# Constant operand for idle products, V0 and V1 in two units each, tile 0 transposed on TensorE, in a scheduled transformer block

## Chip, core and metric

One core of one Trainium2 chip runs the whole program. The metric is the device time in microseconds (us) of an execution, the median of several. Most executions agree within 0.3%, so differences of 0.1 or 0.2 us out of 274 are read from the trace, where single instructions are placed to a few nanoseconds, and only larger ones from the times. PE is TensorE, PEld its weight loads, DVE VectorE, ACT ScalarE, POOL GpSimd, SP the engine that issues most DMAs. PSUM is the memory, in eight banks, that TensorE writes its products to. A "look" is one profiled execution.

## The reference

x is 2048 tokens by 640, taken as 16 tiles of 128 tokens. Cut to what matters:

```python
xn  = layernorm(x)                       # per token, no weights
qkv = xn @ wqkv                          # 640 x 1920; 32 heads of 20
phi = softmax of +-(q @ w_phi), +-(k @ w_phi)   # per head
kv, z = phi_k.T @ v, sum(phi_k)
att = (phi_q @ kv) / (phi_q @ z + 1e-6) @ wo
mlp = (silu(xn @ w1) * (xn @ w3)) @ w2   # 640 -> 1536 -> 640
out = x + att + mlp
```

## The kernel before

The kernel is a program that writes a program. Every instruction is entered with a model duration and its inputs, a list scheduler fixes each engine's order (with random tie-breaking from a seed up to 175 us of model time), and the order is then emitted with semaphore waits. So one edit can move much else.

TensorE is the engine that sets the time. It can't start on real work until x has landed and a tile has been centred, and it starts at half clock; therefore the scheduler fills its first gaps with idle products ("filler"), which nobody reads:

```python
TURNED = (0,)                 # tiles whose normalised rows are transposed by DMA
SEED = 385
...
zero = new("zero", [128, 512], bf, RH + 12288)
...
def consts():
    memset("DVE", warm[:], 0.0, 19)
    memset("DVE", zero[:], 0.0, 9)
    zeroed.append(P.all[-1])
...
def filler(t, until):
    ...
    while t < until:
        cold = t < 5.2
        n = 512 if until - t > 0.5 else 128
        c = n / (1200 if cold else 2400)
        def emit(n=n):
            return nc.tensor.matmul(bank(u.k, n), zero[:, 0:128], zero[:, 0:n], start=True, stop=True)
        P.mm(emit, [], 0, c, n)
        P.all.pop().raw = set(zeroed)      # waits for the memset
        t += c
```

The first four tiles take a short path to V. A tile is centred (`xc`: its mean from an ACT sum, or from DVE's statistics for tile 3), transposed on TensorE (`cT0` to `cT3`), copied from PSUM to `xcT` by ACT or DVE, and multiplied by wv (`V0` to `V3`, ten products of 320 columns each); the copy out of PSUM multiplies by the inverse deviation. Besides, the normalised tiles are transposed into `xnT` (`xT1` to `xT3` on TensorE, tile 0 by DMA). V0 and V1 stand in one piece:

```python
def v_pair(t, level):
    both = P.begin(4, level, stream="V")
    for a, b, u in ((0, 3, 0), (0, 3, 1), (3, DC, 0), (3, DC, 1)):   # chunks a..b of tile t+u
        ...
        for i in range(a, b):
            for q in range(2):
                mm(2 * u + q, ..., xcT[:, t + u, i, :], wv[:, i, 320 * q:320 * q + 320], i == 0, i == DC - 1)
...
P.schedule({"PE": 1.25, "ACT": 1.12, "DVE": 0.93, "POOL": 0.8, "SP": 0.81}, filler, 12.0, SEED, 175.0)
```

The softmax here doesn't subtract the row's maximum and nothing guards it: scores larger than these inputs give would overflow.

## Time and profile before

| | before |
|---|---|
| median time | 274.41 us (3 runs, 274.11 to 274.45) |
| span of the profiled execution | 272.6 us |
| first idle product | 1.29 us |
| clock released (record, and product spacing) | 7.14 us |
| cT0, V0, cT2, V2 start | 4.68, 6.49, 8.98, 10.31 us |
| first MLP product to last product | 14.14 to 269.82 us |

The prediction below shows the shares, the chain and the tile views. One more view: the timeline of the stretch ahead of V2 (columns: start us, length us, engine, line, operation, output<-input, shapes, count, and in brackets the idle time before it and what ended it). These are chosen lines of the kernel before:

```profile
7.33 0.73 ACT L628 ACTIVATE junk<-x_tok 128x640 bf16<-128x640 bf16 x1
...
8.19 0.39 DVE L628 TENSOR_SCALAR xc<-x_tok,mv 128x640 bf16<-128x640 bf16 x1 [0.83 <-ACT junk L628]
...
8.98 0.44 PE L811 MATMUL PS<-ident,xc 128*128 128x128 bf16 x5
...
9.46 0.49 DVE L628 COPY xcT<-PS 128x640 bf16<-128x640 bf16 x1
...
9.80 0.67 PE L1094 MATMUL PS<-zero 128*128 128x128 bf16 x9
...
10.31 1.52 PE L620 MATMUL PS<-wv,xcT 128*128 128x320 bf16 x10
```

Tile 2's sum on ACT, its centring on DVE, its transposes cT2, its copy and V2 form a chain, and TensorE spends the end of it in nine idle products. And V2's operand is copied by 9.95 (9.46 + 0.49) while V2 starts at 10.31: more than half of the idle block comes after the data is there.

### The profile page before, as it was taken

What the parts mean: (1) busy time and instruction counts of PE and PEld (TensorE: products, weight loads), DVE (VectorE), ACT (ScalarE), POOL (GpSimd) and SP (SyncE); (2) the same over time, 40 slices, a digit from 0 to 9 for tenths busy, and PEclk for the clock granted to TensorE, in tenths of its full rate; (3) what the DMA queues carried; (4) which work ended last, traced back from release to release, by engine and by line L of the source; (5) the groups of instructions that cost most, each with busy time, mean ns of one, the idle gap of its engine ahead of it and who ended that gap; (6) DMA issues with size and microseconds to landing.
All of it is one profiled execution on the core that took longest, in us unless ns stands there. A gap on an engine that the chain in (4) does not pass through costs nothing.

```text
span 272.6 us, 5091 instructions
## 1 busy us (share of the span) xinstructions
PE 268.8 (99%) x2099; PEld 159.9 (59%) x2099; DVE 183.8 (67%) x326; ACT 104.2 (38%) x193; POOL 60.5 (22%) x101
## 2 busy tenths in 40 slices
PE   8999999999999999999999999999999999999996
PEld 4747446777754448444444446677677774444774
DVE  5748998999999443588969795677673215666112
ACT  5637754776754540356663354100110002222000
POOL 3320552689999900000000000000000000000000
PEclk9999999999999999999999999999999999999999
DMA  7968996763000000803111111433353222000001
GB/s 233 183 95 258 345 216 129 118 175 114 2 0 2 0 0 10 284 1 46 29 26 24 24 26 25 98 100 96 90 107 83 64 75 72 0 0 0 26 24 48
DMA packets 41959, 22.14 MB, mean 81 GB/s; under 512 B 27728, under 2 KB 41936, under 8 KB 41936
## 3 DMA queue, kind: packets, MB, share of 16 engines
q1 hardware_dynamic: 41360, 21.17, 32.6%
q10 hardware_dynamic: 576, 0.66, 0.7%
q8 instruction: 16, 0.26, 0.4%
q14 instruction: 7, 0.06, 0.1%
HBM read 12.81 MB, written 2.62 MB: 57 GB/s over the span
## 4 chain that ended last, share of the span: by engine, by line
PE 99%; DVE 0%; issue 0%
PE PS L620 96%; PE PS L1094 2%; PE PS L811 1%; PE PS L865 0%; DVE xres L628 0%; DVE zero L628 0%; DVE warm L628 0%
## 5 line engine op out<-in xcount | busy, mean ns | idle before, releaser
L620 PE MATMUL PS<-xnT,w_s 128*128 128x512 bf16 x480 | 106.7, 379 | 0.0
L620 PEld LDWEIGHTS PS<-xnT,w_s 128*128 128x128 bf16 x480 | 46.6, 98 | 55.2
L620 PE MATMUL PS<-w_s,hT 128*128 128x320 bf16 (+2 forms) x384 | 55.0, 300 | 0.0
L628 ACT ACTIVATE th<-PS 128x512 f32<-128x512 f32 x48 | 28.7, 597 | 68.8 <-PE PS L620 68.8
L628 DVE SCALAR_TENSOR_TENSOR t<-th,PS 128x512 bf16<-128x512 f32 x48 | 32.7, 684 | 29.8 <-ACT th L628 29.8
L620 PEld LDWEIGHTS PS<-w_s,hT 128*128 128x128 bf16 x384 | 36.9, 98 | 14.8
L628 POOL TENSOR_TENSOR ekt<-ekt,rS 128x640 bf16<-128x640 bf16 x32 | 39.4, 1268 | 0.7 <-DVE rS L628 0.7
L628 DVE TENSOR_TENSOR xres<-PS,xres 128x640 bf16<-128x640 f32 (+2 forms) x17 | 13.4, 786 | 36.9 <-PE PS L620 36.9
L628 DVE SCALAR_TENSOR_TENSOR hT<-t,PS 128x512 bf16<-128x512 bf16 x48 | 32.7, 683 | 1.3
L628 ACT ACTIVATE EqT<-PS 128x512 bf16<-128x512 f32 x40 | 21.8, 594 | 11.3 <-PE PS L620 11.3
L628 ACT ACTIVATE e_s<-PS 128x64 f32<-128x64 f32 x32 | 9.1, 283 | 40.6 <-PE PS L620 40.1
L620 PE MATMUL PS<-wo_s,oT 128*128 128x320 bf16 (+2 forms) x160 | 24.5, 299 | 0.0
L628 DVE TENSOR_TENSOR prod<-PS,g_s 128x1280 bf16<-128x1280 f32 x16 | 23.9, 1492 | 0.6
L620 PE MATMUL PS<-Wkp,xnT 128*128 128x320 bf16 x160 | 23.9, 299 | 0.0
L628 ACT ACTIVATE ekt<-PS 128x640 bf16<-128x640 f32 x32 | 20.7, 698 | 7.5 <-PE PS L620 7.3
L620 PE MATMUL PS<-xnT,Wqp 128*128 128x512 bf16 x100 | 23.4, 380 | 0.0
L628 DVE TENSOR_REDUCE S<-ekt 128x64 f32<-128x1280 bf16 x16 | 22.9, 1449 | 0.0
L620 PEld LDWEIGHTS PS<-wo_s,oT 128*128 128x128 bf16 x160 | 15.7, 98 | 6.1
L620 PEld LDWEIGHTS PS<-Wkp,xnT 128*128 128x128 bf16 x160 | 15.5, 98 | 5.9
L620 PE MATMUL PS<-wv,xnT 128*128 128x320 bf16 x120 | 18.3, 299 | 0.0
L628 DVE BATCH_NORM_STATS2 bst<-x_tok 128x6 f32<-128x320 bf16 x32 | 13.9, 464 | 2.9 <-DMA x_tok<-in_A_x_dram 2.9
L620 PEld LDWEIGHTS PS<-xnT,Wqp 128*128 128x128 bf16 x100 | 9.3, 98 | 10.8
(68 smaller groups left out, 171.0 us busy)
## 6 DMA issues: line engine op xcount, KB each, us to landing
w_s<-in_B_w_dram SPq DMA_DIRECT2D x8, 480.0 KB, 7.7
xres<-in_A_x_dram SPq DMA_DIRECT2D x16, 160.0 KB, 2.2
out_dram<-xres SPq DMA_DIRECT2D x15, 160.0 KB, 1.8
x_tok<-in_A_x_dram SPq DMA_DIRECT2D x3, 640.0 KB, 7.5
w_s<-in_B_w_dram SPq DMA_DIRECT2D x1, 1920.0 KB, 9.1
wo_s<-in_A_wo_dram SPq DMA_DIRECT2D x1, 800.0 KB, 4.7
x_tok<-in_A_x_dram SPq DMA_DIRECT2D x2, 160.0 KB, 3.4
x_tok<-in_A_x_dram ACTq DMA_DIRECT2D x2, 160.0 KB, 3.8
```

Source lines behind the costliest of these rows:

```text
L620: return nc.tensor.matmul(o(u.k), l, r, start=start, stop=stop, skip_group_check=shared)
L628: return getattr(e, name)(*[at(a, u) for a in args], **{k: at(v, u) for k, v in kw.items()})
L811: return nc.tensor.transpose(PSb[:, a:a + 128], l, ident[:])
L1094: return nc.tensor.matmul(bank(u.k, n), zero[:, 0:128], zero[:, 0:n], start=True, stop=True)
```

## The change

The intent is to get TensorE through its preparation sooner. Idle products read a constant that the preamble sets anyway (1.0, one column per partition, read with step zero), so they wait for nothing and start earlier; V0 and V1 are cut into chunks 0 to 2 and 3 to 4, so that V0 can begin before tile 1 is there; tile 0 goes through TensorE like its neighbours. The core of the diff (a centring mode that is not used, and small changes of model durations, are cut):

```diff
-TURNED = (0,)
-SEED = 385
+TURNED = ()
+SEED = 1023
...
-        memset("DVE", zero[:], 0.0, 9)
-        zeroed.append(P.all[-1])
...
+    ones = nc.const_aps.tensor(1.0, [128, 512], bf)
     def filler(t, until):
-            cold = t < 5.2
-            n = 512 if until - t > 0.5 else 128
-            c = n / (1200 if cold else 2400)
+            n = 512 if until - t > 0.9 else 128
+            c = n / (1200 if t < 6.5 else 2400)
-                return nc.tensor.matmul(bank(u.k, n), zero[:, 0:128], zero[:, 0:n], start=True, stop=True)
+                return nc.tensor.matmul(bank(u.k, n), ones[:, 0:128], ones[:, 0:n], start=True, stop=True)
-            P.all.pop().raw = set(zeroed)
+            P.all.pop()
...
-    v_pair(0, 6e4)
+    v_split(0, 6e4 + 20, 6e4 - 8, 3)      # V0a at this level, V0b at the second
+    v_split(1, 6e4 - 5, 6e4 - 9, 3)
...
-    P.schedule({"PE": 1.25, ...
+    P.schedule({"PE": 0.8, ...
```

The second arguments of `v_split` are levels: a higher level goes first when several units could start.

## The prediction

> **What bounds the kernel now.** I read the page first (shares, then the chain of work that ended last), then that chain in order of time, then the timeline of the first 15 us, then the tile views of that stretch.
>
> ```profile
> PE 268.8 (99%) x2099; PEld 159.9 (59%) x2099; DVE 183.8 (67%) x326; ACT 104.2 (38%) x193; POOL 60.5 (22%) x101
> PE 99%; DVE 0%; issue 0%
> ```
>
> The first line is the page's busy time by engine, the second its chain of work by engine: TensorE sets the end from start to finish. Busy time of pipelined matmuls can hide gaps, so I also added up the start-to-start spacing of the single matmul records. From 14.14 us, where the gated MLP begins, to the last matmul at 269.82 us, spacing beyond columns over 2.4 GHz plus 2.5 ns comes to about 2.2 us; some 1.9 us of it are about twenty steps of 95 ns or so each at the change from whole-array to half-array products, which the change leaves alone. So after 14 us there is nothing to win. Before it, the chain in order of time reads:
>
> ```profile
> 0.96 0.28 DVE zero L628
> 1.29 3.60 PE PS L1094 x11
> 4.88 0.54 PE PS L811 x5
> 5.42 0.74 PE PS L1094 x4
> 6.16 0.53 PE PS L811 x5
> 6.70 2.45 PE PS L620 x16
> 9.15 0.28 PE PS L811 x5
> 9.43 0.54 PE PS L620 x4
> 9.97 0.50 PE PS L1094 x9
> 10.47 1.36 PE PS L620 x10
> 11.83 0.28 PE PS L811 x5
> 12.11 0.84 PE PS L865 x15
> 12.95 119.14 PE PS L620 x945
> ```
>
> Columns: start, length, what. L1094 is the idle products on the zero tile, L811 the transposes of a centred tile (cT0 to cT3), L865 the transposes of normalised tiles 1 to 3, L620 real products (V first). The chain counts by ends, about 0.2 us later than the matmul starts. The reader is to see that TensorE is never empty after 1.29 us, but that two blocks of idle products sit between real work: 0.74 us after cT0 and 0.50 us before V2. Those two blocks, and half speed, are all that can be recovered. Half speed is in the tile views of xc and wv (min/median/max ns):
>
> ```profile
> L811 PE MATMUL PS<-ident,xc x20: 219/267/315, 4.7 to 11.9; 128*128 128x128 bf16 x20
> L620 PE MATMUL PS<-wv,xcT x40: 298/299/475, 6.5 to 14.0; 128*128 128x320 bf16 x40
> ```
>
> A cold 128-column product lasts 315 ns, a warm one 219; the single records are spaced 107 and 56 ns (320 columns: 267 and 136 ns). The clock record and the spacing both change at 7.14 us.
>
> **What the Trainium skill says.** "TensorE: Matmul & The Clock Gate", Part 1, says that the array starts at half clock, that a full busy window of about 3.4 us releases it, and that the window is free-running, so the moment varies from run to run. The trace agrees in size: idle products start at 1.29 us, full speed comes at 7.14 us, 5.85 us later; windows of 3.41 us that end at 7.14 would also end at 3.73, and the one ending there would have been busy only from 1.29. No run yet shows the variation. The same page, "Back-to-back issue gap", gives N/1.2 cold and N/2.4 + 2.5 ns warm: 107 and 56 ns for 128 columns, as measured here. "DMA: Bandwidth & Descriptors", section "DMA Transpose (X-bar)", says that TensorE is the alternative way to transpose, into PSUM, with an identity at hand; this trace shows the price of both: the DMA transpose of tile 0 was issued at 6.52 and landed 6.4 us later, one tile on TensorE takes five products of 56 ns and one copy out of 0.49 us (VectorE) or 0.70 us (ScalarE).
>
> **The change part by part.** As nothing after 14.14 us moves in sum, what counts is the start of the MLP. From the first product of cT0 (4.68) to 14.14 are 9.46 us, and the parts account for them: real work at full speed 35 transposes x 0.056 + 40 V products x 0.136 = 1.96 + 5.43 = 7.39; idle products 0.747 + 0.503 = 1.25; extra for half speed 10 transposes x 0.051 + about 0.32 in the first three V products = 0.83. Sum 9.47.
>
> (a) Idle products without a memset. The zero tile is written by VectorE from 0.96 to 1.24 us (the chain above), and TensorE waits for it until 1.29. A preset constant needs no wait; ScalarE starts at 0.80 and VectorE at 0.88, so I expect TensorE at about 0.85 to 0.9, 0.4 us sooner. This moves no real work: cT0 waits for x (landed 3.15), ScalarE's sum (0.74 + 0.19), and the centring of 0.39, over at 4.42. It brings the release of the clock forward by 0.4 us on average, in steps of 3.4 us depending on the phase. Half of real work's cold time is lost, so about -0.2 us on average, 0 if the phase is as in this trace and the earlier window still is not full. The operand's value and its zero step I count as free.
>
> (b) Finer idle products. cT0's operand is ready at 4.42, cT0 starts at 4.68 behind idle products: about -0.15 with small last ones. cT1's operand is ready at 5.28, and cT1 starts at 5.96: one 427 ns product and three of 107 are too many, because the schedule counted them at full speed from 5.2 us while the chip was at half until 7.14. The new boundary, 6.5 us, and the new size limit, 0.9, should let cT1 start near 5.5. About -0.35; but V0 then waits for the copy of xcT0 (5.45 + 0.49 = 5.94), and its first product will come at 6.1 to 6.2 in place of 6.49, so of the two I keep -0.3 in all.
>
> (c) V0 and V1 in two units each. The old pair had to run as one piece of 20 products after both tiles. Now chunks 0 to 2 of V0 need only xcT0 and wv chunks landed at 4.67 and 5.05; chunks 3 and 4 (landed 6.76 and 7.03) come later. So V0 starts before xcT1 is there, the transposes of tile 2 can go between, and the copies of xcT1 and ScalarE's sum for tile 2 (7.33 to 8.15 before) move up some 0.5 us. That sum ends the wait of VectorE for xc2 (0.83 us idle before 8.19), which fed cT2 at 8.98, whose copy ended at 9.95, which is what V2 waited for behind the 0.50 us of idle products. With cT2 half a microsecond earlier that block should go: -0.5.
>
> (d) Work that moves up lands in the cold time: about 0.35 us of it at half speed, +0.17.
>
> (e) Tile 0 on TensorE: five products, +0.28, and one copy of 0.5 to 0.7 us that stands beside work. The removed DMA transpose landed at 12.88, before the MLP's start, and hid fully; removing it saves TensorE nothing.
>
> Sum: -0.2 - 0.3 - 0.5 + 0.17 + 0.28 = -0.55 us. 274.41 - 0.55 = 273.86; I say 273.9, with the MLP starting near 13.6.
>
> **The rivals.** First, the freed engine work does not reach V2: x tile 2 landed only at 6.14 and tile 3 at 7.27, and VectorE is busy almost without a break from 3.17 us to 13.5. If the copies and statistics come in another order, the 0.5 us block comes back elsewhere, and (e) eats the rest: 274.3 to 274.5. For it speaks that VectorE did 2.46 us of work in the 3.31 us from 6.49 to 9.80; against it, that 0.83 of the rest was one wait for ScalarE. Second, the phase of the clock window decides: with the window just filled by the earlier start, the clock would be free at about 4.3 us, no real product is cold, (d) vanishes and 1 us is won: 273.1 to 273.4. For it, PE starts early enough to fill 0.4 us more of the window; against it, phase is chance, and the three times before lie within 0.34 us of each other, less than a random phase would let me expect. Third, the new seed and the earlier model start reshuffle the order up to 175 us; a list that is off by some hundred nanoseconds against the chip stalls TensorE. Now there is only some 0.15 us of such stalls around 21 to 23 us; if a new list has a bad place, +0.3 to +1 us: 274.5 to 275. Against it, the DMA and the other engines have slack (VectorE 67%, ScalarE 38%).
>
> **Range and chances.** The middle is the sum; the low end is the sum with a favourable window (another 0.7 off), the high end the first rival with a little of the third: 273.1 to 274.6. For 2% the time would have to move 5.5 us, while everything before the MLP that is not real work is 4.9 us of starting time (data not there) and 2.1 us of idle and cold: faster by 2% cannot come from this, slower only from a broken schedule. Faster 0.01, same 0.98, slower 0.01.
>
> **What would show it.** Right: the first idle product near 0.9 us with no VectorE memset before it; V's first product near 6.1; no block of idle products between V1 and V2; five more L865-type transposes, no DMA transpose of tile 0 near 6.5; MLP's first product at 13.4 to 13.8; unchanged length from there to the end, 258.5 us. Wrong: an idle block of half a microsecond at 8 to 12 us, a first MLP product after 14, cold spacing (267 ns) past 7.5 us, or single stalls over 0.2 us inside the MLP stretch.

## The result, and the profile after

The changed kernel took 273.99 us (273.73 to 274.42, 6 runs) against 274.32 us (273.46 to 274.52, 6 runs) for the kernel before. Ratios here divide the mean time of one kernel's fast runs by that of the other's fast runs of the same rounds, so they are not quite the ratio of the medians. This one is 0.9994 with a 95% interval of 0.9979 to 1.001: the same, and no gain resolved. Two controls of the unaltered changed kernel, run later beside experiments, gave 1.0004 (0.9976 to 1.0032) and 0.9991 (0.9973 to 1.001).

In the page of the changed kernel the shares look different, but most of that is missing records:

```profile
PE 267.7 (98%) x2082; PEld 159.9 (59%) x2101; DVE 181.2 (66%) x325; ACT 104.4 (38%) x194; POOL 60.8 (22%) x101
...
PE 94%; ACT 2%; DVE 2%; issue 1%
...
L619 PE MATMUL PS<-xnT,w_s 128*128 128x512 bf16 x465 | 105.1, 379 | 1.1 <-issue 0.3
```

The program has 480 of these MLP products, as before, and the trace has 465 records. Where one is missing, the spacing shows a hole of exactly one product (216 ns), and the chain of work wanders off to ACT or DVE in its place. Allowing for that, the first MLP product, whose own record is missing, starts one V spacing after the last V product: 13.925 + 0.136 = 14.06 us. The last product starts at 269.74. So the stretch from MLP to end is 255.68 us, to 5 ns the same as before, and the whole gain of this execution is 14.14 - 14.06 = 0.08 us. The chain in order of time (start, length, what; L1098 idle products, L814 cT, L867 xT, L619 real products):

```profile
0.84 4.00 PE PS L1098 x15
4.84 0.53 PE PS L814 x5
5.37 0.64 PE PS L1098 x6
6.01 1.27 PE PS L619 x6
7.29 0.28 PE PS L814 x5
7.57 0.54 PE PS L619 x4
8.11 0.04 issue
8.15 0.99 PE PS L619 x6
9.14 0.28 PE PS L814 x5
9.42 0.54 PE PS L619 x4
9.96 0.28 PE PS L867 x5
10.24 1.51 PE PS L619 x10
...
14.28 13.59 PE PS L619 x99
```

Three things are as intended: idle products begin at 0.84, V0's first part (6.01) stands before tile 1's transposes (7.29), and the idle block before V2 is gone. And yet V2 starts at 10.22, 0.09 us earlier than before. The timeline says why:

```profile
4.90 0.39 DVE L627 TENSOR_SCALAR xc<-x_tok,mv 128x640 bf16<-128x640 bf16 x1
...
5.95 1.00 PEld L619 LDWEIGHTS PS<-wv,xcT 128*128 128x128 bf16 x6 [0.20 <-ACT xcT L627]
...
7.12 0.44 PE L814 MATMUL PS<-ident,xc 128*128 128x128 bf16 x5
...
7.60 0.49 DVE L627 COPY xcT<-PS 128x640 bf16<-128x640 bf16 x1 [0.67 <-PE PS L814]
...
8.01 0.38 DVE L627 TENSOR_SCALAR xc<-x_tok,mv 128x640 bf16<-128x640 bf16 x1
...
8.15 0.66 PEld L619 LDWEIGHTS PS<-wv,xcT 128*128 128x128 bf16 x6 [0.37 <-DVE xcT L627]
...
8.98 0.44 PE L814 MATMUL PS<-ident,xc 128*128 128x128 bf16 x5
...
9.46 0.70 ACT L627 ACTIVATE xcT<-PS 128x640 bf16<-128x640 bf16 x1 [0.51 <-PE PS L814]
...
10.22 1.53 PE L619 MATMUL PS<-wv,xcT 128*128 128x320 bf16 x10
```

cT1, whose operand was ready at about 5.3, ran at 7.12, behind V0a. So xcT1 was copied at 8.09, V1a waited for it (0.37 us of idle weight loads), cT2 came at 8.98 as in the kernel before, although its operand was ready at 8.4, and V2 waited for its copy. That copy had also changed its engine: ACT took 0.70 us, to 10.16, where DVE had taken 0.49, to 9.95. So the idle block went, but 0.21 us of what that freed went to the slower copy. With a copy as short as before, V2 could have followed the five transposes of tile 0, at 10.08 (an estimate from the product spacing; no run moved this copy back). From V2's start to MLP's start TensorE then has the same 3.84 us of work in both kernels.

The working of the prediction from cT0 to MLP, redone on the changed kernel (single records): real work 40 transposes x 0.056 + 40 V products x 0.136 = 7.67; six idle products 0.64; three holes without any product, before V0a, V1a and V2, 0.15 + 0.21 + 0.14 = 0.50; cold extra 0.26 for five transposes and 0.35 for three V products = 0.61. The sum is 9.42 against 9.43 measured (4.633 to 14.061); the kernel before had 7.39 + 1.25 + 0.83. Idle products became holes, and the five new transposes took the rest.

### The profile page after: what moved, and what is told of

It reads as the page before. It is cut to its first block, busy times and chain, and to the rows that moved or that the text cites. A ratio compares the mean times of both kernels' runs of the same rounds, so it can differ in the third digit from the quotient of the medians.

```text
span 272.5 us, 5069 instructions
## 1 busy us (share of the span) xinstructions
PE 267.7 (98%) x2082; PEld 159.9 (59%) x2101; DVE 181.2 (66%) x325; ACT 104.4 (38%) x194; POOL 60.8 (22%) x101
## 4 chain that ended last, share of the span: by engine, by line
PE 94%; ACT 2%; DVE 2%; issue 1%
PE PS L619 92%; ACT EqT L627 2%; PE PS L1098 2%; DVE S L627 1%; DVE rS L627 1%; PE PS L814 1%; PE PS L867 0%; DVE Wqp L627 0%; DVE xres L627 0%
## 5 line engine op out<-in xcount | busy, mean ns | idle before, releaser
L619 PE MATMUL PS<-xnT,w_s 128*128 128x512 bf16 x465 | 105.1, 379 | 1.1 <-issue 0.3
L619 PEld LDWEIGHTS PS<-xnT,w_s 128*128 128x128 bf16 x480 | 46.4, 98 | 54.6
L619 PE MATMUL PS<-w_s,hT 128*128 128x320 bf16 (+2 forms) x384 | 55.0, 299 | 0.0
L619 PEld LDWEIGHTS PS<-w_s,hT 128*128 128x128 bf16 x384 | 37.1, 98 | 14.9
L627 DVE TENSOR_TENSOR xres<-PS,xres 128x640 bf16<-128x640 f32 (+2 forms) x17 | 13.4, 786 | 40.8 <-PE PS L619 40.8
L619 PE MATMUL PS<-wo_s,oT 128*128 128x320 bf16 (+2 forms) x160 | 24.5, 299 | 0.0
L619 PE MATMUL PS<-Wkp,xnT 128*128 128x320 bf16 x160 | 23.9, 299 | 0.0
L619 PE MATMUL PS<-xnT,Wqp 128*128 128x512 bf16 x96 | 22.9, 380 | 0.3 <-issue 0.2
L619 PEld LDWEIGHTS PS<-wo_s,oT 128*128 128x128 bf16 x160 | 15.7, 98 | 6.1
L619 PEld LDWEIGHTS PS<-Wkp,xnT 128*128 128x128 bf16 x160 | 15.5, 98 | 5.9
L619 PE MATMUL PS<-wv,xnT 128*128 128x320 bf16 x120 | 18.3, 299 | 0.0
L619 PEld LDWEIGHTS PS<-xnT,Wqp 128*128 128x128 bf16 x100 | 9.3, 98 | 10.8
```

Of the source, the lines that this page charges most:

```text
L619: return nc.tensor.matmul(o(u.k), l, r, start=start, stop=stop, skip_group_check=shared)
L627: return getattr(e, name)(*[at(a, u) for a in args], **{k: at(v, u) for k, v in kw.items()})
```

## The experiments

My theory after the result: (1) the gain at V2 was lost because cT1 was put behind V0a; (2) tile 0's five transposes cost nothing, as they stand in V2's wait; (3) the clock is released a fixed 5.85 us after the first product, since both profiles show exactly that (1.29 to 7.14 and 0.84 to 6.69). Rivals: the split itself, or the seed, or weights that land late, or DVE's chain is what holds V2; and for (3), a window that runs free of the kernel's start.

Rescheduling after every edit would move everything else too. So most experiments keep the scheduler's result: the order of each engine is frozen, single instructions are taken out, put in or moved, and the waits are derived anew from the data and PSUM dependences. A build of the frozen kernel without edits gave the same order on every engine. All variants gave correct results.

### Idle products on the zero tile again

```diff
+    ones = zero tile, memset by DVE after warm
+    every idle product waits for that memset
-    the first idle product of 512 columns
```

> The changed kernel with its instruction order frozen, but the idle products read the zero tile again, wait for its memset, and the first long one is dropped so that cT0 stays near 4.65 us. Theory (the clock is released a fixed 5.85 us after the first product, as in both profiles: 1.29 to 7.14 and 0.84 to 6.69): release at 7.14, about 0.45 us more of V0 at half speed, MLP's first product at 14.28 in place of 14.06, time +0.2 us on the changed kernel. Rival (the window runs free of the kernel's start, the two equal distances are chance): release anywhere between 4.7 and 8.1 us, MLP's start not tied to it by 0.2 us.

Measured: 274.08 us, ratio to before 0.9999 (0.9956 to 1.0042). First product at 1.29, but the clock released at 4.02 us, 2.73 us after it. The theory of a fixed distance fell with the first look. The rival's idea stood, but not its range: 4.02 lies before the 4.7 that I had set as the earliest, because I had taken a full window as needed. And there was a second lesson: here no real product ran cold, x landed 0.28 us later than in the changed kernel's profile (DVE's first statistics at 3.46 in place of 3.18), and MLP started at 13.99 in place of 14.06. A clock released 2.7 us sooner (4.02 against 6.69) came with a V2 only 0.08 us sooner. Late data had a part in that: besides x, the last weights of V landed at 7.76 only, and V0b's last two products waited for them until 7.80.

### The idle products alone, in the kernel before

```diff
 kernel before, order frozen
-    memset of the zero tile and the waits for it
+    idle products on the constant 1.0, one more of 512 columns in front
```

> The kernel before with its order frozen and only one part of the change: idle products on the preset constant, no memset, one long idle product more so that cT0 stays near 4.64 us. Theory: first product at 0.84, release at 6.69, V's first products cold for 0.45 us less, MLP at 13.92 in place of 14.14: this part alone wins all that the whole change won (0.08 us in the profile) and more, so the other parts together cost 0.1 us. Rival (the idle products' part is worth nothing, the split did it): release and MLP's start as before, 7.14 and 14.14.

Measured: 273.90 us, ratio 0.9992 (0.9955 to 1.0028). First product at 0.84, release at 6.34, V2 at 10.08, MLP at 13.91 in place of 14.14. The position of MLP came out as expected, partly by luck: the release came 0.80 us sooner than before, 0.35 more than the start did, and one look can't say how much of the 0.80 is due to the start at all and how much to the phase of the window. In its profile this part alone does better than the whole change (13.91 against 14.06). The times don't resolve such a difference.

### No idle products at all

```diff
 changed kernel, order frozen
-    all 21 idle products
```

> The changed kernel, order frozen, with no idle products at all: TensorE first works at cT0, near 4.5 us. Theory (fixed distance): release near 10.3 us, all of V0 and V1 at half speed, MLP at 15.3 to 15.6, time +1.3 to +1.5 us. Rival (free-running window of 3.41 us): release anywhere between 7.9 and 11.3 us. Second rival (idle products are worth nothing because the data waits hide the cold clock): time as the changed kernel.

Measured: 275.17 us, ratio 1.0048 (1.0009 to 1.0088). First product 4.55, release at 9.20, so 4.65 us later: neither fixed nor beyond the rival's range. V0 began at 5.84, and V2 came at 11.16 and MLP at 15.01, 0.95 us later than with idle products. They are worth about 1 us to this kernel by the profiles, less than the 1.3 to 1.5 I had put on them, as the release came 1.1 us sooner than I had set. The times agree: the interval of this ratio excludes 1. The second rival (idle products worth nothing) is out.

### Tile 0 by DMA again

```diff
 changed kernel, order frozen
-    xT0: five transposes on PE, one copy on DVE
+    one DMA transpose on SP behind the first MLP weights
```

> The changed kernel, order frozen, with tile 0 transposed by DMA again (five products and one copy out less, one DMA transpose more). Prediction's step (e): tile 0 on TensorE costs 0.28 us, so MLP at 13.78. Theory now: the five products stand in the wait of V2 for the copy of xcT2 (9.80 to 10.22 us in the changed kernel's profile), so V2 still starts at 10.2 and MLP at 14.06, difference 0 to 0.05 us; VectorE has 0.48 us less to do and gains nothing on the end.

Measured: 274.25 us, ratio 1.0006 (0.9969 to 1.0042); V2 at 10.28, MLP at 14.12. Without the five products nothing came sooner. The chain of this run in order of time shows that V2 waits for the copy on ACT, not for TensorE:

```profile
1.25 4.98 DMA wv<-in_A_wqkv_dram
6.23 0.14 issue
...
9.20 0.29 PE PS L814 x5
9.50 0.02 issue
9.52 0.71 ACT xcT L627
10.23 0.05 issue
10.28 1.53 PE PS L619 x10
```

It also shows a new limit on V0's early start: in this execution the first weights of V landed at 6.23 us only, and V0 started at 6.37 in place of 5.96. The prediction's +0.28 for tile 0 is thus wrong in the changed kernel, because its products stand in a wait.

### cT1 first

```diff
 changed kernel, order frozen
-    PE:  cT0, 6 idle, V0a, cT1, V0b, V1a, cT2, V1b, xT0, V2
+    PE:  cT0, 1 idle, cT1, V0a, V0b, V1a, cT2, V1b, xT0, V2
-    DVE: apply0, aggr1, stats2, copy xcT1
+    DVE: copy xcT1, apply0, aggr1, stats2
```

> The changed kernel, order frozen but for two moves: the transposes of tile 1 (cT1) go before V0's first part (as the prediction had assumed), with one idle product left ahead of them, and VectorE copies xcT1 before it normalises tile 0. Theory: the gain that the prediction put on the block before V2 was lost because cT1 stands behind V0a, so that xcT1 is copied at 8.09 only, V1a and cT2 wait for that (cT2 at 8.98, as before the change), and V2 waits for the copy of xcT2. With cT1 first: cT1 at 5.4, xcT1 copied at 6.6, cT2 near 8.5, V2 at 9.7 in place of 10.2, MLP at 13.5 to 13.8 (14.06), from MLP's start to the last product 255.68 us as in all runs so far, time 0.3 to 0.5 us under the changed kernel. Rival (VectorE's chain for tile 3 or a landing of weights binds anyway): V3 not before 12.6, MLP at 14.0.

Measured: 274.00 us, ratio 0.9976 (0.9951 to 1.0001). V2 at 9.75, MLP at 13.59, 0.47 us ahead of the changed kernel's profile. The edit is one package: cT1's place, five idle products less, and the copy of xcT1 earlier on DVE; the shares of the three were not separated. Run again beside a control of the changed kernel:

> The same kernel as the run with cT1 first, beside the control on one chip: 0.3 to 0.5 us under the control, MLP at 13.5 to 13.7. If the gain in that run was only an early clock release or luck, it lies within 0.15 us of the control.

Measured: 273.72 us, ratio 0.9997 (0.9970 to 1.0024), beside the control

> The changed kernel unaltered, as the control on the same chip. Expected: 0.0 to 0.35 us under the kernel before; MLP's first product 13.9 to 14.2, varying with the moment of the clock's release (so far from 2.7 to 5.9 us after the first product) and with the landing of x and of the V weights; 255.7 us from there to the last product.

with 274.20 us, 1.0004. MLP stood at 13.25 here (record missing, one spacing after the last V product) and at 14.22 in the control. The means of the six runs are 273.87 and 274.11, so 0.24 us, less than the 0.3 to 0.5 expected and not resolved: single runs of the first reach from 273.53 to 274.74. In both looks at this kernel the clock happened to be released early (spacing turns near 4.7 and 4.4 us), so part of the distance to the control is chance. The fair partner is the zero-tile run, with the old order, a release at 4.02 and MLP at 13.99. In it and in the first look V0b waited for its last weights (landed at 7.76 and 7.37), which leaves 0.40 us for the order at an early clock. In the second look these weights had landed by 6.98 and nothing waited for them, so its 0.74 us holds the luck of an early landing too.

The lines of the timeline for the first look, which answer to those of the changed kernel:

```profile
5.75 0.45 PE L814 MATMUL PS<-ident,xc 128*128 128x128 bf16 x5 [0.53 <-ACT xcT L627]
...
6.24 0.49 DVE L627 COPY xcT<-PS 128x640 bf16<-128x640 bf16 x1 [0.15 <-PE PS L814]
...
8.51 0.44 PE L814 MATMUL PS<-ident,xc 128*128 128x128 bf16 x5
...
8.99 0.70 ACT L627 ACTIVATE xcT<-PS 128x640 bf16<-128x640 bf16 x1 [0.30 <-PE PS L814]
```

xcT1 is copied at 6.73 in place of 8.09 and cT2 runs at 8.51 in place of 8.98. One thing is not as I wrote: cT1 starts at 5.75 and not at 5.4, released by ACT's copy of xcT0. It has cT0's PSUM bank. In the changed kernel this cost nothing, since cT1 came late anyway.

### cT1 first, and tile 0 by DMA

> As the run before, and tile 0 transposed by DMA again. Theory: V2 has no wait worth 0.28 us any more, so here the five products count, or VectorE's copy of 0.48 us does: MLP at 13.4 to 13.6, 0.1 to 0.3 us under the run before. Rival: tile 0 on TensorE is free here too, no difference.

The edit is the sum of the two. Measured: 274.02 us, ratio 0.9979 (0.9954 to 1.0005). Release at 5.94, MLP at 13.54: inside the range that I expected, but only 0.05 us before the run with cT1 first; so the rival, no difference, describes it better. V2 waited for the copy of xcT2 here too (0.42 us by the spacing), so the five transposes were free again: from cT2's start to V2's it is 1.24 us in both runs. And the stretch from MLP to the last product grew to 255.94: one hole of 0.26 us at 20.2 us, in the products that fold w_phi into wk. Whether the extra DMA transpose or MLP's earlier start causes it was not tested.

### The old seed

```diff
-SEED = 1023
+SEED = 385
```

> The changed kernel with the old seed 385, rescheduled: cT1 behind V0a here too (the levels put it there, not the seed), tile 0's transposes before V1a, and six short idle products before V2. Theory: only the first 14 us can differ; V2 at 10.2 to 10.4, MLP at 14.05 to 14.25, and 255.68 us from there to the last product. Rival (the seed's order up to 175 us matters): that length differs by more than 0.1 us.

Measured: 274.44 us, ratio 0.9989 (0.9957 to 1.0021). V2 at 10.04, MLP at 14.01, both a little before the range that I expected, with the clock released at 4.65; 255.85 us from there to the end. The old seed also has cT1 behind V0a: the levels put it there. The end stretch is 0.17 us longer, more than my limit of 0.1: most steps from whole-array to half-array products cost 95 ns, but three of them 166 to 175, against two such in the kernel before, which accounts for 0.08 us; the other 0.10 is one step back to whole-array products, at 141.24 us, of 191 ns in place of 95. So the seed does matter after 14 us, but by 0.17 us.

### A better order

```diff
 changed kernel, order frozen
+    PE:   cT0, 1 idle, cT1, V0a, V1a, V0b, cT2, V1b, xT0, V2
+    ACT:  copy of xcT2 before the copy of V0
+    PSUM: V2, cT3, xT0 to xT3 in other banks, so that none should wait for the copies of V0 and V1
```

> The run with cT1 first, and besides: V1's first part before V0's second (which waited 0.28 us for its weights), the transposes of tile 2 before V1's second part with their copy ahead of V0's copy on ScalarE, and PSUM banks of V2, cT3 and the late transposes chosen so that none waits for V0's or V1's copy. Theory: V2 at 9.3 to 9.5, MLP at 13.1 to 13.4, 0.3 us under the run with cT1 first. Rival: VectorE's chain (tile 3's statistics, normalising of tiles 2 and 3, end near 11.3, then xcT3's copy) holds V3 at 12.1 or later, and MLP stays at 13.5.

Measured: 273.72 us, ratio 0.9993 (0.9968 to 1.0018), mean 273.75 against 274.11 for the control of the same chip. V2 at 9.96 and MLP at 13.80 (one spacing after the last V product), not 13.1 to 13.4. The rival did not apply: V3 came behind V2's work with no wait of its own. The clock was released at 6.63, so both cT0 and cT1 were cold, and cT1 had to wait for cT0's bank until 5.95; V0 started at 6.46. So the last run gave cT1 a bank of its own, next to a second control:

```diff
+    PSUM: cT1 in bank 7 in place of bank 0
```

> The changed kernel unaltered, a second control beside the next run: 0 to 0.3 us under the kernel before, MLP between 13.9 and 14.25.

> As the run with the new order, and cT1 in a PSUM bank of its own: in the runs with cT1 first it stood in cT0's bank and waited for the copy of xcT0 (it started at 5.69 to 5.99 and not at 5.4). Theory: cT1 at 5.4, done before xcT0 is copied, so V0 starts at 5.95 to 6.2 even with the clock cold; V2 at 9.3 to 9.6, MLP at 13.15 to 13.45, 0.5 to 0.8 us under the control on the same chip. Rival: VectorE's chain for tile 3 binds next and MLP stays at 13.5 or later.

Measured: the control 274.01 us, 0.9991, MLP at 14.11; the new kernel 273.70 us, ratio to before 0.9977 with an interval of 0.9961 to 0.9994, which excludes 1. The means of six runs are 273.65 and 274.08, so 0.43 us; I had expected 0.5 to 0.8. Of the thirteen ratios here only this one and that of the run without idle products have intervals that exclude 1. Its chain:

```profile
5.48 0.56 PE PS L814 x5
6.04 0.09 issue
6.13 2.33 PE PS L619 x16
8.47 0.29 PE PS L814 x5
8.76 0.54 PE PS L619 x4
9.30 0.28 PE PS L867 x5
9.58 1.51 PE PS L619 x10
```

cT1 begins at 5.39 (the chain counts by ends, so it shows 5.48), V0 at 6.13, V2 at 9.55, MLP at 13.49 (0.04 above the range that I expected). Most of what was left before V2 is now work. V3 waited some 0.08 us: VectorE's copy of xcT3 ended at 12.06 and V3 began at 12.12. The rival, that DVE's chain binds next, is beginning to be true. V0's first weights landed at 6.00 here, 0.13 us before V0 began; they were as late in two more looks (6.08 in the first control, 6.23 in the run with tile 0 by DMA) and were there by 5.4 in all others. This landing is the other thing that varies from look to look.

All looks side by side (us; "first" is the first product; where MLP's own record is missing, one V spacing after the last V product is given):

| kernel | first | clock released | after first | cT1 | V2 | MLP | ratio to before |
|---|---|---|---|---|---|---|---|
| before | 1.29 | 7.14 | 5.85 | 5.96 | 10.31 | 14.14 | |
| changed | 0.84 | 6.69 | 5.85 | 7.12 | 10.22 | 14.06 | 0.9994 |
| changed, control 1 | 0.84 | 6.76 | 5.92 | 7.28 | 10.37 | 14.22 | 1.0004 |
| changed, control 2 | 0.84 | 6.74 | 5.90 | 7.15 | 10.27 | 14.11 | 0.9991 |
| zero tile | 1.29 | 4.02 | 2.73 | 6.62 | 10.14 | 13.99 | 0.9999 |
| before, constant 1.0 | 0.84 | 6.34 | 5.50 | 5.91 | 10.08 | 13.91 | 0.9992 |
| no idle products | 4.55 | 9.20 | 4.65 | 7.42 | 11.16 | 15.01 | 1.0048 |
| tile 0 by DMA | 0.84 | 6.43 | 5.59 | 7.19 | 10.28 | 14.12 | 1.0006 |
| seed 385 | 0.84 | 4.65 | 3.81 | 6.50 | 10.04 | 14.01 | 0.9989 |
| cT1 first | 0.84 | near 4.7 | 3.8 | 5.75 | 9.75 | 13.59 | 0.9976 |
| cT1 first, again | 0.84 | near 4.4 | 3.6 | 5.69 | 9.40 | 13.25 | 0.9997 |
| cT1 first, tile 0 by DMA | 0.84 | 5.94 | 5.10 | 5.99 | 9.69 | 13.54 | 0.9979 |
| better order | 0.84 | 6.63 | 5.78 | 5.96 | 9.96 | 13.80 | 0.9993 |
| better order, own bank | 0.84 | 5.84 | 5.00 | 5.39 | 9.55 | 13.49 | 0.9977 |

The column "MLP" sorts by the place of cT1: all six looks with cT1 behind V0a and with idle products lie from 13.99 to 14.22, and all five of the changed kernel with cT1 moved ahead from 13.25 to 13.80, whatever the clock did (released from 4.02 to 6.76 us in the first group, from 4.4 to 6.63 in the second). The comparison holds within the split kernel alone: the kernel before has cT1 early too, but its V0 and V1 in one piece.

## Why the prediction was right or wrong

The number was right: 273.9 predicted, 273.99 measured. That says little for the reasons, since the range, 273.1 to 274.6, held the unchanged kernel's 274.32 as well. The place of MLP tells more: 13.6 was predicted and 14.06 came, and "a first MLP product after 14" was one of the prediction's own signs of being wrong. Of the reasons, some held.

- **What bounds it** held. All that the change can move is the start of MLP; from there to the last product it is 255.68 us in the kernel before, the changed one, its two controls and four of the experiments, and up to 0.26 us more in the others. The prediction's sum of stalls there is one-sided: its some twenty steps of 95 ns (1.9 us) are those from whole-array to half-array products, and the steps back cost as much, so the trace has 35 and 3.5 us in all. They are there in both kernels.
- **(a)** held in mechanism. The first product came at 0.84 with no memset (predicted 0.85 to 0.9). The cold extra fell from 0.83 to 0.61, the 0.2 us predicted; but the release is a matter of phase, and that both profiles have 5.85 us is chance. The free-running window that the prediction took from "TensorE: Matmul & The Clock Gate", Part 1, of the Trainium skill agrees with the table, 2.73 to 5.92 us after the first product; that it must be full does not (the last section).
- **(b)** failed at "should let cT1 start near 5.5". V0 did start early (5.96, better than the 6.1 to 6.2 predicted), and cT0 came 0.04 sooner instead of 0.15. But cT1 did not move up; it moved back, to 7.12, because V0a has the higher level in the diff. I had read those numbers and still assumed cT1 first. And 5.5 was out of reach for a second reason: in the changed kernel cT1 shares cT0's PSUM bank, so that even when it came first it started at 5.69 to 5.99, and at 5.39 only with a bank of its own.
- **(c)** failed for that reason: "With cT2 half a microsecond earlier that block should go: -0.5". The block of idle products went, cT2 stayed at 8.98, and V2 gained 0.09: of the 0.36 us that the idle products had held V2 back, most went to a copy of xcT2 that was 0.21 us slower on ACT. The runs with cT1 first show the predicted step in its place: cT2 at 8.17 to 8.51 and V2 at 9.40 to 9.75 in the two looks at that kernel.
- **(d)** was mis-sized: the extra half-speed work of +0.17 did not appear as a net rise. V0a's early products did run cold (0.35 us extra), but cT1, now late, ran warm.
- **(e)** failed: "+0.28" for tile 0 on TensorE. The products are there (40 transposes in place of 35), but inside V2's wait, and taking them out gained nothing (MLP 14.12 against 14.06, 14.11 and 14.22). "Removing it saves TensorE nothing" did hold.
- **The first rival** named the outcome best, that the block comes back elsewhere, though not the time (274.3 to 274.5). Its cause was another, TensorE's own order and not DVE's. **The second rival** (an early clock wins 1 us) fell: released at 4.02 and 4.65 us, V2 came at 10.14 and 10.04. In both looks waits for data, late weights among them, took up most of what the warm clock saved: in the first, the holes without a product before V2 sum to 1.18 us, against 0.50 in the changed kernel. **The third**, the seed, is worth 0.17 us after 14 us, not 0.3 to 1.

In the sums from cT0 to MLP, idle products and holes fell only from 1.25 to 1.14 us (0.64 + 0.50), where (b) and (c) had put -0.8; the cold extra fell by 0.22, where (a) and (d) together had put -0.03; and tile 0's products filled what would have been a wait. So errors of opposite sign partly cancelled, and in the profile the change gains 0.08 us, not 0.55; that the median still fell on 273.99 is luck, within the spread of single runs (273.73 to 274.42).

## What to carry to other kernels

When a unit is cut so that it can start earlier, look at what it now stands in front of: V0a had the higher level, and the transposes that fed everything after it came 1.8 us after they were ready, though they take half a microsecond even cold. Before a term is put on the sum, ask whether the engine waits at that place anyway: five products in a wait cost nothing, and a warm clock before a wait gains little. A schedule that moves a copy to a slower engine can take back what the order gave. And where only a prologue can change, follow its one chain to the start of the steady part; here a few moves in the order and other PSUM banks gave what the parts of the change had not (0.9977 against 0.9991 on one chip).

## What the Trainium skill lacked or had wrong

- "TensorE: Matmul & The Clock Gate", Part 1, asks for a busy window of about 3.4 us, "sustained". In the zero-tile run the clock was released 2.73 us after the first product, so, if the release falls at a window's end, a window filled to 80% (2.73 of 3.41) was enough. In the first control the window that ended 5.92 - 3.41 = 2.50 us after the first product did not release it (73%). The bound lies between, if windows follow each other without a gap; in all twelve clock records on hand the time from release to the drop after the end is 266.24 or 269.65 us, two lengths that differ by 3.413 us and are 78 and 79 times that.
- The same page puts the change "around 4µs", give or take 500 ns. Here it came 2.7 to 5.9 us after the first product, in fourteen looks (in two of them read from the spacing).
- The same page, Part 4, says that full clock doesn't engage for transposes and that one took about 275 ns in a kernel. Here transposes (`nc.tensor.transpose` in the kernel) after the release last 219 ns and are spaced 56 ns, like any 128-column product. Whether transposes alone would release the clock was not tested.
- The same page, "Back-to-back issue gap", gives 81 ns for 128 columns and 131 ns for 512 as the sustained rate of weight load and product pairs. Here such streams run at 56 and 216 ns, the page's figures for the isolated gap.
- No page that I found gives the cost of a one-column constant read with step zero as both operands of a product. Its cold spacing is 427 ns for 512 columns and 107 ns for 128, the same as with the zero tile.
